# Attention and two dense layers in one program: scores kept negated, fewer small steps, three tiles of each early pair turned by TensorE

## The chip, the cores and the metric

The program runs on one core of a Trainium2 chip. The time is device microseconds for one execution. The core has TensorE (PE; its weight loads are shown apart as PEld), VectorE (DVE), ScalarE (ACT), GpSimd (POOL) and SyncE (SP), which here issues all DMAs. Each engine runs its own instructions in the order in which the program has them; semaphores make one wait for another.

## What is computed

Attention over 4 batches of 8 heads (576 positions, 64 columns a head), in which scores further than `tau` below the row's maximum are dropped, and behind it two dense layers over all 2304 rows (512 to 2048 and back), the first with `s * relu(h)^2 + b`, the second with `h * sigmoid(1.702 h)`:

```python
scores = scale * np.matmul(q, k.transpose(0, 1, 3, 2))
thresh = np.max(scores, axis=-1, keepdims=True) - tau
scores = np.where(scores >= thresh, scores, -1000000000.0)
scores = scores - np.max(scores, axis=-1, keepdims=True)
attn = np.exp(scores)
attn = attn / (np.sum(attn, axis=-1, keepdims=True) + 1e-09)
x = np.matmul(attn, v)                      # then heads side by side
g = s * np.maximum(x @ w_in, 0.0) ** 2 + b  # first layer, x = g @ w_out
h = x @ w_in2; out = (h / (1.0 + np.exp(-1.702 * h))) @ w_out2
```

## The kernel before

*Attention.* Two heads make a pair; 16 pairs, four to a batch, each with nine score tiles of 128 rows (`tile_step`, tile 8 holds the last 64 rows of both heads). TensorE multiplies a tile's scores into a PSUM buffer `S` of 128x576, of which there are three while the first batch runs, two later. VectorE takes the row's negated maximum (`nm`, line 511) and derives from it `tb`, the bound below which a score is dropped (line 516), and `nb`, the bias of the exponential (line 522). ScalarE computes `e = exp(S + nb)` (line 529). VectorE masks it with `S >= tb` and sums the row in the same instruction (line 533), after which `S` is free. ScalarE rounds `e` to 16 bits (`p16`, line 324), GpSimd puts the rest into the second half of `p16` (lines 542 and 543), and SP issues a DMA transpose of `p16` into `PT` (line 545). With all nine tiles of a pair turned, TensorE multiplies them with the values (`finish_main`, line 605, `finish_last`, line 646) into a PSUM buffer `T`, which is also used for smaller transposes; there are two of these in the first batch. Values are scaled by a power of two for each head (`prep_v`, lines 444 to 450: reduction, four small steps on `vm`, two copies into `vcol`, reciprocal).

*Dense layers.* All matmuls of the two layers write `y` (line 788 for the hidden rows, 851 for the projection). The weights arrive as 64-bit numbers and are first converted (`convert`: ScalarE, three instructions on VectorE, one on GpSimd for each block of 128 rows). The first batch's rows of the first layer run with 32-bit matmuls, the others with three products of shorter ones. The layers of a batch start as soon as that batch's attention is done, and run interleaved with the attention of the later batches; from about 710 us on only `y` matmuls are left on TensorE.

*What sets the order.* Every step is put into a `Plan` with its engine, an estimated cost, its buffers and a priority from a table of constants `KN` (times at which parts are due, and leads in us). `Plan.run` goes through the steps in order of time and gives each free engine the ready step of the lowest priority value; the resulting order is written out as it is. What SP, VectorE, ScalarE, GpSimd and TensorE do one after another is thus fixed when the program is built.

Of the kernel before, what the change touches and what calls it, by code (L numbers as in the profile page):

```python
# [9 lines left out]
F32 = mybir.dt.float32  # L10
F32R = mybir.dt.float32r
F16 = mybir.dt.float16
# [14 lines left out]
R = 9  # L27
# [17 lines left out]
    "spread": 8,  # L45
}

# [22 lines left out]
class Plan:  # L70
# [50 lines left out]
    def run(self, engines):  # L121
        steps = self.steps
        for op in steps:
            op["left"] = len(op["after"])
            for a in op["after"]:
                steps[a]["then"].append(op["n"])
        slots = {k: q[0].bufs for k, q in self.turns.items()}
        next_turn = dict.fromkeys(self.turns, 0)
# [3 lines left out]
        clock = Clock()  # L132
        for seg in range(self.segment + 1):
# [7 lines left out]
            while count < len(todo):  # L141
# [4 lines left out]
                while ends and ends[0][0] <= now:  # L146
                    for b in steps[heapq.heappop(ends)[1]]["bufs"]:
                        b.users -= 1
                        if b.users == 0:
                            slots[id(b.pool), b.tag] += 1  # L150
                moved = False
                for e in engines:
# [3 lines left out]
                    while ready[e]:  # L156
# [12 lines left out]
                        need = {}  # L169
                        ok = True  # L170
                        new = sorted((b for b in op["bufs"] if not b.live), key=lambda b: b.turn)
                        for b in new:
                            k = (id(b.pool), b.tag)
                            i = need.get(k, 0)
                            if b.turn != next_turn[k] + i or slots[k] <= i:
                                ok = False
                                break
                            need[k] = i + 1
                        if not ok:
                            put.append((p, n))  # L180
                            continue
                        for b in new:
                            b.live = True
                        for k, i in need.items():
                            next_turn[k] += i
                            slots[k] -= i
                        op["start"], op["on"] = now, e
# [94 lines left out]
class Kernel:  # L282
# [9 lines left out]
    def consts(self, pool):  # L292
        nc = self.nc
        self.ident = pool.tile([P, P], F32, name="ident")
        make_identity(nc, self.ident)
        sc = pool.tile([P, 3], F32, name="scal")
# [12 lines left out]
        self.under = pool.tile([P, 1], F32, name="under")  # L309
        nc.vector.tensor_tensor(self.under, t1, t2, ALU.add)  # L310
# [44 lines left out]
    def ps(self, tag, shape):  # L355
# [5 lines left out]
        return Buf(self.pa if own else self.px, tag, shape, F32, n if own else more)  # L361
# [55 lines left out]
    def prep_v(self, p):  # L417
# [24 lines left out]

        def scales(_):
# [7 lines left out]
        add({"DVE": 1085.0}, scales, [T], [vm, vs, vcol])  # L451
# [11 lines left out]
    def tile_step(self, p, i):  # L463
# [38 lines left out]
        else:  # L502
# [4 lines left out]
        tb = self.at("tb", [P, 1], F32, bufs=4)  # L507
# [3 lines left out]
            {"DVE": 668.0}, lambda _: nc.vector.tensor_reduce(nm.ap, Sv(), AX.XY, ALU.max, negate=True), [Sp], [nm],  # L511
# [3 lines left out]
            {"DVE": 130.0},  # L515
            lambda _: nc.vector.tensor_scalar(tb.ap, nm.ap, -1.0, self.under, ALU.mult, ALU.subtract), [nm], [tb],  # L516
            prio=self.plan.prio - KN["tb"] * pace,
        )
        nb = self.at("nb", [P, 1], F32, bufs=4)
        add(  # L520
            {"DVE": 130.0},
            lambda _: nc.vector.tensor_scalar(nb.ap, nm.ap, LOG_SP, None, ALU.add), [nm], [nb],
            prio=self.plan.prio - KN["tb"] * pace - 1.0,
# [5 lines left out]
            lambda _: nc.scalar.activation(ev(), Sv(), AF.Exp, bias=nb.ap, scale=1.0), [Sp, nb], [e],  # L529
# [4 lines left out]
                ev(), Sv(), tb.ap, ev(), ALU.is_ge, ALU.mult, accum_out=p["acc"][:, i, 0:1]  # L534
            ),
            [Sp, tb, e], [e, (p["acc"], i)], prio=self.plan.prio - KN["sc"] * pace,
# [8 lines left out]
        add({"SP": (1360.0, 1800.0, 1280.0)}, lambda _: nc.sync.dma_start_transpose(pt(), p16.ap), [p16], [(PT, part)], turns=True)  # L545
# [116 lines left out]
    def attention(self, pairs):  # L662
# [3 lines left out]
        for n, p in enumerate(pairs):  # L666
# [3 lines left out]
            def do(step, p, i):  # L670
                at = pairs[n]["start"] + pairs[n]["pace"] * i / R
                plan.prio, self.lending = at, p["lend"]
                step(p)

            if n == 0:
                do(self.prep_qk, p, 0)
            p["PT"] = {}
# [23 lines left out]
    def heads(self, b, start, pace, lend=False):  # L701
        return [
            {
                "b": b, "hp": hp, "start": start + hp * pace, "pace": pace, "lend": lend,
                "parts": b * NP + hp >= KN["parts"], "spread": b * NP + hp >= KN["spread"],
            }
            for hp in range(NP)
        ]
# [383 lines left out]
```

## Time and profile before

| what | us |
|---|---|
| median of 3 runs | 1100.98 (1099.6 to 1103.26) |
| the profiled execution | 1097.05 |
| its span in the trace | 1095.2 |
| TensorE busy in the span | 1034.4 |
| VectorE busy in the span | 810.4 |
| ScalarE busy in the span | 675.6 |

The page's busy time of TensorE counts a matmul from its start to its modelled end, at whatever clock it ran. The table of stretches gives for each engine how long it was busy in a window, the number of instructions in brackets, and the granted clock as a share of the full 2.4 GHz. The list of waits gives an engine and a line, and the engine and line whose end ended the wait. The timeline's first two columns are start and duration in us.

### The profile page before, as it was taken

To read this page: it belongs to the slowest core of one execution; us is meant where nothing else is said; L and a number is where in the kernel's file an instruction comes from. 1 tells how busy PE (TensorE), PEld (TensorE's weight loads), DVE (VectorE), ACT (ScalarE), POOL (GpSimd) and SP (SyncE) were. 2 spreads that over 40 slices of the span, in tenths; PEclk is the share of its full clock that TensorE was granted. 3 is DMA by queue.
4 is the path that set the end of the run, shared out by engine and by line. 5 is a ranking of instruction groups with operands and counts; after the bars stand their busy time and mean duration, and the time that the engine had idled before them with its cause. 6 is when DMAs were issued, how large, how long until landed. Compare 5 with 4: busy or idle time off the path is not lost.

```text
span 1095.2 us, 16161 instructions
## 1 busy us (share of the span) xinstructions
PE 1034.4 (94%) x5264; PEld 754.5 (69%) x5264; DVE 810.4 (74%) x1727; ACT 675.6 (62%) x1216; POOL 430.6 (39%) x477
## 2 busy tenths in 40 slices
PE   3777889999999999999999999999999999999998
PEld 1333334445678777878877787868888888888886
DVE  6999798999898988999998878765444544444443
ACT  5776778778988765776666587655655433223221
POOL 2765565757775577556556343500000000000000
PEclk7777899999999998999999999999999999999999
DMA  7999899898988656768576866542211112020102
GB/s 220 202 188 225 217 244 247 211 255 239 227 197 227 165 136 171 204 170 223 139 187 162 198 171 145 127 139 78 78 60 66 30 49 68 1 68 10 54 34 67
DMA packets 228756, 161.54 MB, mean 147 GB/s; under 512 B 180728, under 2 KB 181312, under 8 KB 228672
## 3 DMA queue, kind: packets, MB, share of 16 engines
q1 hardware_dynamic: 228672, 160.52, 57.3%
q8 instruction: 41, 0.67, 0.3%
q14 instruction: 43, 0.35, 0.1%
HBM read 93.85 MB, written 24.15 MB: 108 GB/s over the span
## 4 chain that ended last, share of the span: by engine, by line
PE 56%; DVE 6%; issue 2%; ACT 1%; DMA 1%; SPq 0%; POOL 0%; DVEq 0%; ACTq 0%; POOLq 0%
PE y L851 27%; PE y L788 26%; PE S L490 2%; PE T L605 1%; DVE e L533 1%; DVE ww L749 1%; DVE nm L511 1%; DVE gl L339 1%; DVE ww L738 0%; DVE wl L339 0%; DMA wst<-in_moe_w_in 0%; DVE accb L864 0%; DVE wa L742 0%; DMA raw<-in_q 0%; DVE gt L816 0%
## 5 line engine op out<-in xcount | busy, mean ns | idle before, releaser
L542 POOL TENSOR_TENSOR p<-e,p 128x512 f16<-128x512 f32 x123 | 151.3, 1230 | 150.7 <-ACT p L324 122.1
L788 PE MATMUL y<-xa,wh 128*128 128x512 f32 x512 | 183.8, 453 | 0.0
L788 PE MATMUL y<-xb,wh 128*128 128x512 f32 x512 | 164.0, 401 | 0.4 <-DVE xb L339 0.4
L851 PE MATMUL y<-gh,wh 128*128 128x512 f32 (+1 forms) x384 | 156.1, 449 | 3.3 <-POOL wh L759 2.0
L529 ACT ACTIVATE e<-S,nb 128x576 f32<-128x576 f32 x144 | 104.3, 733 | 46.0 <-DVE tb L516 19.9
L533 DVE SCALAR_TENSOR_TENSOR e<-S,tb,e 128x576 f32<-128x576 f32 x144 | 115.8, 808 | 15.3 <-ACT e L529 14.3
L788 PEld LDWEIGHTS y<-xa,wh 128*128 128x128 f32 x512 | 94.0, 190 | 43.4 <-issue 26.7
L851 PE MATMUL y<-wh,gh 128*128 128x512 f32 x288 | 115.6, 401 | 3.7 <-DVE gt L816 3.7
L511 DVE TENSOR_REDUCE nm<-S 128x1 f32<-128x576 f32 x144 | 106.4, 745 | 14.5 <-PE S L497 8.0
L851 PE MATMUL y<-wl,gh 128*128 128x512 f32 x288 | 114.4, 397 | 0.0
L851 PE MATMUL y<-wh,gl 128*128 128x512 f32 x288 | 114.3, 397 | 0.0
L813 ACT ACTIVATE gt<-y 128x512 f32<-128x512 f32 (+1 forms) x80 | 44.2, 553 | 111.1 <-PE y L788 111.0
L339 DVE TENSOR_TENSOR gl<-gt,gh 128x512 fp32r<-128x512 f32 (+1 forms) x134 | 99.4, 757 | 17.7 <-ACT gh L324 17.0
L788 PEld LDWEIGHTS y<-xb,wh 128*128 128x128 f32 x512 | 94.9, 189 | 24.5 <-DVE xb L339 1.3
L816 DVE SCALAR_TENSOR_TENSOR gt<-gt,y 128x512 f32<-128x512 f32 (+1 forms) x80 | 50.4, 630 | 75.7 <-ACT gt L813 75.7
L788 PE MATMUL y<-xb,wl 128*128 128x512 f32 x256 | 101.6, 397 | 0.0
L324 ACT ACTIVATE p<-e 128x576 f16<-128x576 f32 x123 | 82.8, 678 | 30.5 <-DVE e L533 20.7
L339 POOL TENSOR_TENSOR gl<-gt,gh 128x512 fp32r<-128x512 f32 (+1 forms) x10 | 11.9, 1190 | 222.0 <-DVE gh L320 220.8
L851 PEld LDWEIGHTS y<-gh,wh 128*128 128x128 f32 x384 | 70.7, 189 | 37.1 <-issue 23.2
L851 PE MATMUL y<-gl,wh 128*128 128x512 f32 (+1 forms) x256 | 93.8, 366 | 0.5 <-POOL gl L339 0.5
L851 PE MATMUL y<-gh,wl 128*128 128x512 f32 (+1 forms) x256 | 93.8, 366 | 0.0
L324 ACT ACTIVATE wh<-wl 128x512 fp32r<-128x512 f32 x104 | 64.1, 626 | 33.6 <-DMA wl<-wd 32.2
(138 smaller groups left out, 2193.1 us busy)
## 6 DMA issues: line engine op xcount, KB each, us to landing
wl<-wd SPq DMA_DIRECT2D x128, 256.0 KB, 2.9
wst<-in_moe_w_in SPq DMA_DIRECT2D x32, 512.0 KB, 4.7
wst<-in_moe_w_out SPq DMA_DIRECT2D x32, 512.0 KB, 5.0
wd<-wh SPq DMA_DIRECT2D x32, 256.0 KB, 4.2
wd<-ww SPq DMA_DIRECT2D x32, 256.0 KB, 2.1
raw<-in_k SPq DMA_DIRECT2D x16, 288.0 KB, 3.1
raw<-in_q SPq DMA_DIRECT2D x16, 288.0 KB, 3.0
rv<-in_v SPq DMA_DIRECT2D x14, 320.0 KB, 5.5
```

Of the source, the lines that this page charges most:

```text
L324: nc.scalar.activation(dst(), src(), AF.Copy)
L339: engines, lambda e: self.eng[e].tensor_tensor(dst(), a(), b(), ALU.subtract), reads, writes, **kw
L490: nc.tensor.matmul(Sp[:, half, :HALF], q[h][j][:, qcols[h]], k[h][:, half * HALF : (half + 1) * HALF], start=(h, j) == (heads[0][0], 0), s ...
L511: {"DVE": 668.0}, lambda _: nc.vector.tensor_reduce(nm.ap, Sv(), AX.XY, ALU.max, negate=True), [Sp], [nm],
L529: lambda _: nc.scalar.activation(ev(), Sv(), AF.Exp, bias=nb.ap, scale=1.0), [Sp, nb], [e],
L533: lambda _: nc.vector.scalar_tensor_tensor(ev(), Sv(), tb.ap, ev(), ALU.is_ge, ALU.mult, accum_out=p["acc"][:, i, 0:1]),
L542: nc.gpsimd.tensor_tensor(p16[:, S + H2 :], e[:, :MAIN], p16[:, :MAIN], ALU.subtract)
L605: nc.tensor.matmul(Up[h * H2 : (h + 1) * H2, :], V[:, h, slot, :], p["PT"][h][:, j, :], start=start, stop=stop)
L788: nc.tensor.matmul(hp(), wt[:, kk * P : (kk + 1) * P], xv(j, kk), start=(i == 0), stop=(i == len(terms) - 1))
L813: add({"ACT": act(n, True)}, lambda _: nc.scalar.activation(t(), hp(), AF.Tanh, scale=0.851), [hps], [gt])
L816: lambda _: nc.vector.scalar_tensor_tensor(t(), t(), 1.0, hp(), ALU.add, ALU.mult), [hps, gt], [gt],
L851: nc.tensor.matmul(yp(), a, b, start=(i == 0), stop=(i == len(terms) - 1))
```

## The change

The scores are kept negated: the scale of `k` has the other sign, so the row's minimum is taken, the exponential gets a scale of -1, and the mask asks `<=`. Bias and bound come from one instruction: a constant tensor `both` of 128x3 (bias, bound, zero) plus the row's minimum gives `nb`, of which column 0 is the bias and column 1 the bound. The scaling of values takes both heads in one instruction, and the copies into `vcol` move to GpSimd. In each pair of the first batch, tiles 1, 8 and 6 (by `TURNS[1]`, twelve tiles in all) are turned by TensorE: nine 128x128 transposes of 16-bit numbers into two `T` buffers, five and four, each copied to `PT` by ScalarE. `s` and `b` are loaded behind the first pair's loads, a `warm` activation is added on ScalarE, and an identity of 16 bits on GpSimd. The table `KN` has other numbers, which move instructions on all engines, and `Plan.run` keeps a step that waits for a buffer aside until one comes free.

```diff
-    "lead": 6, "boost": 30, "mix": 14, "ahead": 10, "t0": 59.94, "t1": 186.71, "t2": 461.81, "t3":
+    "lead": 2, "boost": 45, "mix": 14, "ahead": 4, "t0": 57.56, "t1": 186.71, "t2": 430.13, "t3":
...
+TURNS = ((), (1, 8, 6), (0, 2, 8, 5, 7), (8,), (1, 6))
...
-        for i, src in enumerate((self.tau, self.s, self.b)):
-            nc.sync.dma_start(sc[:, i : i + 1], src.partition_broadcast(P))
-        self.s_ap, self.b_ap = sc[:, 1:2], sc[:, 2:3]
+        nc.sync.dma_start(sc[:, :1], self.tau.partition_broadcast(P))
+        self.warm = pool.tile([P, 1], F32, name="warm")
+        nc.scalar.activation(self.warm, self.ident[:, :1], AF.Exp)
...
-        nc.vector.tensor_scalar(self.qs, z, 1.0 / math.sqrt(D), None, ALU.mult)
+        nc.vector.tensor_scalar(self.qs, z, -1.0 / math.sqrt(D), None, ALU.mult)
...
+        self.both = pool.tile([P, 3], F32, name="both")
+        nc.vector.memset(self.both, 0.0)
+        nc.vector.tensor_scalar(self.both[:, 0:1], t2, 0.0, LOG_SP, ALU.mult, ALU.add)
+        nc.vector.tensor_tensor(self.both[:, 1:2], t1, t2, ALU.add)
+
+    def layer_consts(self):
+        for i, src in enumerate((self.s, self.b)):
+            self.nc.sync.dma_start(self.sc[:, i + 1 : i + 2], src.partition_broadcast(P))
...
         def scales(_):
-            nc.vector.tensor_reduce(vm.ap, T.ap, AX.X, ALU.max)
-            for h in range(2):
-                m, rows = vm[:, h : h + 1], slice(h * H2, (h + 1) * H2)
-                nc.vector.tensor_scalar(m, m, 2.0 ** -113 / unit, unit, ALU.max, ALU.mult)
-                nc.vector.tensor_scalar(m.bitcast(I32), m.bitcast(I32), 0x7F800000, None, ALU.bitwise_and)
-                nc.vector.tensor_copy(vcol[rows], m[rows])
-            nc.vector.reciprocal(vs.ap, vm.ap)
+            m = vm.ap.bitcast(I32)
+            nc.vector.tensor_scalar(vm.ap, vm.ap, 2.0 ** -113 / unit, unit, ALU.max, ALU.mult)
+            nc.vector.tensor_scalar(m, m, 0x7F800000, None, ALU.bitwise_and)
+            nc.vector.reciprocal(vs.ap, vm.ap)
+        add({"DVE": 450.0}, scales, [vm], [vm, vs])
+
+        def col(e):
+            for h in range(2):
+                rows = slice(h * H2, (h + 1) * H2)
+                self.eng[e].tensor_copy(vcol[rows], vm[rows, h : h + 1])
+        add({"POOL": 300.0}, col, [vm], [vcol])
...
-            {"DVE": 668.0}, lambda _: nc.vector.tensor_reduce(nm.ap, Sv(), AX.XY, ALU.max, negate=True), [Sp], [nm],
+            {"DVE": 668.0}, lambda _: nc.vector.tensor_reduce(nm.ap, Sv(), AX.XY, ALU.min), [Sp], [nm],
...
-            lambda _: nc.vector.tensor_scalar(tb.ap, nm.ap, -1.0, self.under, ALU.mult, ALU.subtract), [nm], [tb],
+            lambda _: nc.vector.tensor_scalar(nb.ap, self.both, nm.ap, None, ALU.add), [nm], [nb],
...
-            lambda _: nc.vector.tensor_scalar(nb.ap, nm.ap, LOG_SP, None, ALU.add), [nm], [nb],
...
-            lambda _: nc.scalar.activation(ev(), Sv(), AF.Exp, bias=nb.ap, scale=1.0), [Sp, nb], [e],
+            lambda _: nc.scalar.activation(ev(), Sv(), AF.Exp, bias=nb[:, 0:1], scale=-1.0), [Sp, nb], [e],
...
-                ev(), Sv(), tb.ap, ev(), ALU.is_ge, ALU.mult, accum_out=p["acc"][:, i, 0:1]
+                ev(), Sv(), nb[:, 1:2], ev(), ALU.is_le, ALU.mult, accum_out=p["acc"][:, i, 0:1]
...
+        for some in (range(KS), range(KS, R)):
+            T = self.ps("T", [P, KS, P], F16)
+
+            def turn(_, some=some, T=T):
+                for j in some:
+                    nc.tensor.transpose(T[:, j - some[0], :], p16[:, j * P : (j + 1) * P], self.ident16)
+            add({"PE": (len(some) * 60.0 + 100.0, 60.0)}, turn, [p16], [T])
+            self.copy(
+                lambda some=some: pt()[:, some[0] : some[-1] + 1], lambda some=some, T=T: T[:, : len(some)], [T],
+                [(PT, (part, some[0]))], len(some) * P, psum=True, also=0,
+            )
```

Three places show what moves. SP's queue at the very start, before:

```order
L298 DMA scal<-in_tau 128x1
L298 DMA scal<-in_moe_s 128x1
L298 DMA scal<-in_moe_b 128x1
L343 DMA kk<-in_k 128x576
L343 DMA qa<-in_q 128x576
L343 DMA qb<-in_q 128x576
```

and SP's queue at the same place in the changed program:

```order
L311 DMA scal<-in_tau 128x1
L366 DMA kk<-in_k 128x576
L366 DMA qa<-in_q 128x576
L366 DMA qb<-in_q 128x576
L366 DMA rv<-in_v 128x640
L333 DMA scal<-in_moe_s 128x1
L333 DMA scal<-in_moe_b 128x1
```

The two loads of one number now stand behind the four large ones of the first pair.

VectorE in the first pair, around the masks of its sixth and seventh tile, before (`nm` is the row's maximum, `e` the masked exponential, `ww` and `wa` steps of a weight's conversion):

```order
L511 TENSOR_REDUCE nm_277<-S_255 128x1
L742 TENSOR_SCALAR wa_205<-ww_266 128x65x8
L522 TENSOR_SCALAR nb_285<-nm_277 128x1
L516 TENSOR_SCALAR tb_287<-nm_277,under_87 128x1
L533 SCALAR_TENSOR_TENSOR e_279,acc_110<-S_225,tb_275,e_279 128x576
L511 TENSOR_REDUCE nm_292<-S_270 128x1
L533 SCALAR_TENSOR_TENSOR e_290,acc_110<-S_255,tb_287,e_290 128x576
L522 TENSOR_SCALAR nb_304<-nm_292 128x1
L516 TENSOR_SCALAR tb_306<-nm_292,under_87 128x1
```

and VectorE there in the changed program, from the mask of the seventh tile on:

```order
L557 SCALAR_TENSOR_TENSOR e_281,acc_114<-S_255,nb_277,e_281 128x576
L541 TENSOR_REDUCE nm_298<-S_284 128x1
L541 TENSOR_REDUCE nm_306<-S_291 128x1
L546 TENSOR_SCALAR nb_314<-both_89,nm_298 128x3
L546 TENSOR_SCALAR nb_322<-both_89,nm_306 128x3
L541 TENSOR_REDUCE nm_324<-S_301 128x1
L784 TENSOR_SCALAR wa_203<-ww_273 128x65x8
L546 TENSOR_SCALAR nb_341<-both_89,nm_324 128x3
L557 SCALAR_TENSOR_TENSOR e_326,acc_114<-S_284,nb_314,e_326 128x576
```

Each tile has one small instruction where there were two, and reductions stand further ahead of the masks.

ScalarE at the end of the first pair, before (`e` the exponential of a tile's scores, `gt` and `p16` its 16-bit copy, `wa` a weight's conversion):

```order
L529 ACTIVATE e_315<-S_270,nb_304 128x576
L732 ACTIVATE wa_329<-wst_138 128x64x8
L733 ACTIVATE wa_329<-ident_70 128x8
L529 ACTIVATE e_333<-S_296,nb_325 128x576
L324 ACTIVATE gt_340<-e_315 128x576
L324 ACTIVATE gt_349<-e_333 128x576
```

and ScalarE there in the changed program (`T` is what TensorE has turned of the fifth tile):

```order
L347 ACTIVATE p16_304<-e_281 128x576
L553 ACTIVATE e_326<-S_284,nb_314 128x576
L347 ACTIVATE PTm_333<-T_316 128x640
L347 ACTIVATE PTm_333<-T_328 128x512
L553 ACTIVATE e_344<-S_291,nb_322 128x576
L347 ACTIVATE gt_348<-e_326 128x576
```

The two copies of turned numbers stand between the exponentials of the eighth and the ninth tile.

## Rows read from the trace of the kernel before

**Rows 1.** The page: span, and busy time (share of span) of each engine.

```profile
span 1095.2 us, 16161 instructions
PE 1034.4 (94%) x5264; PEld 754.5 (69%) x5264; DVE 810.4 (74%) x1727; ACT 675.6 (62%) x1216; POOL 430.6 (39%) x477
```

**Rows 2.** Table of stretches: window, length, engines' busy time, TensorE's clock, DMA share, GB/s.

```profile
0.00:20.00 20.00, 6.80 (x30) 3.35 (x30) 10.35 (x33) 10.10 (x18) 3.87 (x12) 0.89 0.69 235
20.00:113.00 93.00, 69.15 (x443) 32.84 (x442) 89.51 (x269) 68.74 (x118) 60.30 (x82) 0.73 0.93 203
113.00:160.00 47.00, 41.07 (x165) 17.00 (x164) 39.32 (x96) 36.25 (x69) 26.46 (x32) 0.89 0.90 234
160.00:345.00 185.00, 181.82 (x831) 101.74 (x830) 168.12 (x362) 154.63 (x287) 122.19 (x130) 1.00 0.90 230
345.00:720.00 375.00, 365.45 (x1906) 289.40 (x1905) 330.87 (x668) 253.44 (x450) 210.71 (x217) 0.99 0.69 172
720.00:1095.00 375.00, 370.16 (x1896) 310.19 (x1894) 172.24 (x304) 152.47 (x279) 7.03 (x7) 1.00 0.17 53
```

**Rows 3.** Timeline, the last matmul.

```profile
1090.13 0.40 PE L851 MATMUL y<-wl,gh 128*128 128x512 f32 x1
```

**Rows 4.** Waits from 20 to 113 us: total us, times, longest.

```profile
PE S L497 <- DVE e L533: 13.8, 13, 2.1
ACT e L529 <- DVE tb L516: 12.0, 11, 3.4
```

**Rows 5.** Stretches again, VectorE's instructions that write or read `nm`.

```profile
0.00:20.00 20.00, 4.24 (x11) 0.89 0.69 235
20.00:113.00 93.00, 34.92 (x117) 0.73 0.93 203
```

**Rows 6.** Timeline of the start: `s` and first `k`, table load, first scores.

```profile
1.18 0.42 SPq L298 DMA_DIRECT2D scal<-in_moe_s  x1
...
2.12 0.43 SPq L343 DMA_DIRECT2D kk<-in_k  x1
...
6.49 1.28 ACT L379 ACT_TABLE_LOAD   x1 [6.49 <-DMA kk<-in_k]
...
8.61 3.25 PE L497 MATMUL S<-kk,qa 64*128 64x288 f32 x12 [8.61 <-ACT kk L379]
```

**Rows 7.** Timeline, VectorE, the two small steps of a tile and their successor.

```profile
31.60 0.15 DVE L522 TENSOR_SCALAR nb<-nm 128x1 f32<-128x1 f32 x1
31.67 0.21 DVE L516 TENSOR_SCALAR tb<-nm,under 128x1 f32<-128x1 f32 x1
31.79 0.17 DVE L552 TENSOR_REDUCE ri<-acc 128x9 f32<-128x18 f32 x1
```

**Rows 8.** Timeline, VectorE, the first step on `vm` and the successor of the last.

```profile
37.24 0.15 DVE L447 TENSOR_SCALAR vm<-vm 128x1 f32<-128x1 f32 x1
...
38.29 0.80 DVE L533 SCALAR_TENSOR_TENSOR e<-S,tb,e 128x576 f32<-128x576 f32 x1
```

**Rows 9.** Who waited for the DMA transposes of line 545 (us, times), whole run.

```profile
  PE T L605: 1.6, 2
...
  ACT p L324: 0.5, 1
```

**Rows 10.** A copy out of PSUM (grouped, 20 to 113 us); two groups of matmuls (timeline).

```profile
L324 ACT ACTIVATE rs<-T 64x512 f32<-64x512 f32 x8 | 4.7, 588 | 1.1 <-PE T L580 0.9
...
720.36 0.63 PE L646 MATMUL T<-PTm,V 128*64 128x64 f16 x28
...
132.96 0.60 PE L580 MATMUL T<-ident,ri 128*64 128x128 f32 x4
```

**Rows 11.** Timeline, GpSimd, the larger step of a tile's low part.

```profile
139.21 1.16 POOL L542 TENSOR_TENSOR p<-e,p 128x512 f16<-128x512 f32 x1 [1.36 <-issue]
```

**Rows 12.** Timeline, scores of one tile at the upper and the lower clock.

```profile
118.70 0.76 PE L497 MATMUL S<-kk,qb 64*128 64x288 f32 x4
...
125.18 1.33 PE L497 MATMUL S<-kk,qa 64*128 64x288 f32 x4 [1.73 <-DVE e L533]
```

More of the change, by code (lines that the diff above doesn't have):

```diff
@@ L40 @@
 KN = {
[4 rows of a table removed]
-    "spread": 8,
[4 rows of a table added]
+    "turns": 1, "tn": 4, "spread": 8,
 }
+TURNS = ((), (1, 8, 6), (0, 2, 8, 5, 7), (8,), (1, 6))
 class Buf:
@@ L126, in run @@
                 steps[a]["then"].append(op["n"])
+            op["keys"] = [((id(b.pool), b.tag), b) for b in sorted(op["bufs"], key=lambda b: b.turn)]
         slots = {k: q[0].bufs for k, q in self.turns.items()}
+        blocked = {k: [] for k in slots}
         next_turn = dict.fromkeys(self.turns, 0)
@@ L132, in run, with again @@
         clock = Clock()
+        def again(k):
+            for e, p, n in blocked[k]:
+                heapq.heappush(ready[e], (p, n))
+            blocked[k].clear()
         for seg in range(self.segment + 1):
@@ L146, in run @@
                 while ends and ends[0][0] <= now:
-                    for b in steps[heapq.heappop(ends)[1]]["bufs"]:
+                    for k, b in steps[heapq.heappop(ends)[1]]["keys"]:
                         b.users -= 1
                         if b.users == 0:
-                            slots[id(b.pool), b.tag] += 1
+                            slots[k] += 1
+                            again(k)
                 moved = False
@@ L168, in run @@
                                 continue
[L169 to L173, printed above, removed]
+                        need, stuck = {}, None
+                        for k, b in op["keys"]:
+                            if b.live:
+                                continue
                             i = need.get(k, 0)
                             if b.turn != next_turn[k] + i or slots[k] <= i:
-                                ok = False
+                                stuck = k
                                 break
                             need[k] = i + 1
-                        if not ok:
-                            put.append((p, n))
+                        if stuck:
+                            blocked[stuck].append((e, p, n))
                             continue
-                        for b in new:
+                        for k, b in op["keys"]:
                             b.live = True
@@ L186, in run @@
                             slots[k] -= i
+                            again(k)
                         op["start"], op["on"] = now, e
@@ L295, in consts @@
         make_identity(nc, self.ident)
+        self.ident16 = pool.tile([P, P], F16, name="ident16")
+        nc.gpsimd.tensor_copy(self.ident16, self.ident)
         sc = pool.tile([P, 3], F32, name="scal")
-        for i, src in enumerate((self.tau, self.s, self.b)):
-            nc.sync.dma_start(sc[:, i : i + 1], src.partition_broadcast(P))
-        self.s_ap, self.b_ap = sc[:, 1:2], sc[:, 2:3]
+        nc.sync.dma_start(sc[:, :1], self.tau.partition_broadcast(P))
+        self.warm = pool.tile([P, 1], F32, name="warm")
+        nc.scalar.activation(self.warm, self.ident[:, :1], AF.Exp)
+        self.s_ap, self.b_ap, self.sc = sc[:, 1:2], sc[:, 2:3], sc
         z = pool.tile([P, 1], F32, name="z")
@@ L308, in consts @@
         nc.vector.tensor_scalar(t2, sc[:, 0:1], 0.0, None, ALU.max)
-        self.under = pool.tile([P, 1], F32, name="under")
-        nc.vector.tensor_tensor(self.under, t1, t2, ALU.add)
+        self.both = pool.tile([P, 3], F32, name="both")
[5 more added lines that the diff above has]
+            self.nc.sync.dma_start(self.sc[:, i + 1 : i + 2], src.partition_broadcast(P))
     def copy(self, dst, src, reads, writes, cols, scale=None, psum=False, also=0, **kw):
@@ L353, in at, with ps @@
         return Buf(self.ap, tag, shape, dt, bufs)
-    def ps(self, tag, shape):
+    def ps(self, tag, shape, dt=F32):
         n, more = {"S": (2, 1), "T": (1, 1)}[tag]
@@ L360, in ps @@
         own = i % (n + more) < n
-        return Buf(self.pa if own else self.px, tag, shape, F32, n if own else more)
+        return Buf(self.pa if own else self.px, tag, shape, dt, n if own else more)
     def prep_qk(self, p):
@@ L441, in prep_v @@
         vs = self.at("vs", [P, 2], F32)
+        add(
+            {"DVE": dve(256, psum=True) + 60}, lambda _: nc.vector.tensor_reduce(vm.ap, T.ap, AX.X, ALU.max), [T], [vm]
+        )
         def scales(_):
-            nc.vector.tensor_reduce(vm.ap, T.ap, AX.X, ALU.max)
-            for h in range(2):
-                m, rows = vm[:, h : h + 1], slice(h * H2, (h + 1) * H2)
-                nc.vector.tensor_scalar(m, m, 2.0 ** -113 / unit, unit, ALU.max, ALU.mult)
-                nc.vector.tensor_scalar(m.bitcast(I32), m.bitcast(I32), 0x7F800000, None, ALU.bitwise_and)
-                nc.vector.tensor_copy(vcol[rows], m[rows])
-            nc.vector.reciprocal(vs.ap, vm.ap)
-        add({"DVE": 1085.0}, scales, [T], [vm, vs, vcol])
+            m = vm.ap.bitcast(I32)
[4 more added lines that the diff above has]
+        def col(e):
+            for h in range(2):
+                rows = slice(h * H2, (h + 1) * H2)
+                self.eng[e].tensor_copy(vcol[rows], vm[rows, h : h + 1])
+        add({"POOL": 300.0}, col, [vm], [vcol])
         for h in range(2):
@@ L514, in tile_step @@
         add(
-            {"DVE": 130.0},
-            lambda _: nc.vector.tensor_scalar(tb.ap, nm.ap, -1.0, self.under, ALU.mult, ALU.subtract), [nm], [tb],
+            {"DVE": 150.0},
+            lambda _: nc.vector.tensor_scalar(nb.ap, self.both, nm.ap, None, ALU.add), [nm], [nb],
             prio=self.plan.prio - KN["tb"] * pace,
[L518 to L521, printed above, removed]
-            lambda _: nc.vector.tensor_scalar(nb.ap, nm.ap, LOG_SP, None, ALU.add), [nm], [nb],
-            prio=self.plan.prio - KN["tb"] * pace - 1.0,
         )
@@ L544, in tile_step @@
         add({"POOL": Shared(pool(MAIN) + pool(H2))}, low, [e, (p16, 0)], [(p16, 1)])
-        add({"SP": (1360.0, 1800.0, 1280.0)}, lambda _: nc.sync.dma_start_transpose(pt(), p16.ap), [p16], [(PT, part)], turns=True)
+        if i not in p["turns"]:
+            add(
+                {"SP": (1360.0, 1800.0, 1280.0)}, lambda _: nc.sync.dma_start_transpose(pt(), p16.ap), [p16], [(PT, part)],
+                turns=True,
+            )
+            return
+        for some in (range(KS), range(KS, R)):
[7 more added lines that the diff above has]
+                [(PT, (part, some[0]))], len(some) * P, psum=True, also=0,
+            )
     def finish_sums(self, p):
@@ L676, in attention @@
                 do(self.prep_qk, p, 0)
+                plan.add({"SP": 1040.0}, lambda _: self.layer_consts(), prio=1.0)
             p["PT"] = {}
@@ L703, in heads @@
             {
+                "turns": TURNS[KN["turns"]] if b * NP + hp < KN["tn"] else (),
                 "b": b, "hp": hp, "start": start + hp * pace, "pace": pace, "lend": lend,
```

4 lines of the change are left out of this document (2 added, 2 removed), and 6 rows, old and new, of the table KN.

## The prediction

> **What bounds the kernel now.** I read the page's first line, then the table of stretches, then who waits for whom inside the stretch that looked worst, and last the timeline at the places that the change touches. TensorE is busy for 1034.4 of 1095.2 us [rows 1], so the span is TensorE's work plus its idle time plus what it loses to the lower clock. The stretches say where that is [rows 2]. After 160 us TensorE idles 3.2 us up to 345, 9.6 us up to 720 and 4.8 us to the end, of which the last sum and the stores after the last matmul take 4.7 (the last matmul ends at 1090.53) [rows 3]. Before 160 us it idles 13.2 us (0 to 20), 23.9 us (20 to 113) and 5.9 us (113 to 160), at a granted clock of 0.89, 0.73 and 0.89 against 1.00 later. Whatever this change gives must come from there, about 43 us of idle time and some slow matmuls.
>
> In 20 to 113 us VectorE is busy for 89.5 of 93 us, and what TensorE waits for there is the score buffer that VectorE's masking step frees (13.8 us in 13 waits) [rows 4]. ScalarE's exponentials wait for VectorE's small step `tb` (12.0 us) [rows 4]. So the first stretch is VectorE's. By 113 us some 42 of the 144 score tiles have been reduced (11 + 117 instructions on `nm`, three for each tile) [rows 5]. From 113 to 345 us it is mixed: TensorE is nearly full (222.9 of 232 us), VectorE at 207.4 of 232 [rows 2].
>
> **The change, part by part.** The profiled execution took 1097.05 us and its span is 1095.2; the median of the runs shown is 1100.98, 3.9 us more. I sum against 1097.05 and add the 3.9 at the end.
>
> *Head.* The loads of `s` and `b` leave the front of SP's queue. They were issued at 1.18 and 1.64, and `kk` behind them at 2.12 [rows 6]; `kk` can now go at about 1.18, 0.94 us earlier. The chain from it is single: landing, table load, scaling, first scores at 8.61 [rows 6]. The new `warm` activation, which would take the 1.28 us table load out of that chain, stands in ScalarE's program behind the table load and the first `kk` scaling, and the table load still waits for the same DMA, so I give it nothing. Head: -0.9 us.
>
> *Small steps.* `nb` starts at 31.60, `tb` at 31.67, the next instruction at 31.79: the pair holds VectorE for 0.19 us [rows 7]. One step with a tensor operand remains; no row shows it. Its ends are 0.07 us (like `nb`) and 0.19 us (nothing saved). I take 0.12, the time from `tb` to its successor, because `tb` too reads an operand from memory: 0.07 us saved for each tile. Keeping the scores negated is free: the reduction and the mask keep shape and source.
>
> *Scales.* Behind the reduction of `vm` come seven small instructions from 37.24 until the next one starts at 38.29: 1.05 us [rows 8]. Three remain, each on the result of the one before: 3 of 7 by count, 0.45 us. Saved 0.6 us for each pair of heads. The two copies to `vcol` go to GpSimd, which has 32.7 us idle in 20 to 113 [rows 2], and are read a pair later.
>
> To tile 42 this is 42 x 0.07 + 5 x 0.6 = 5.9 us of VectorE. The order of the program moves conversions of weights around that: ahead of tile 37 it now has eight more of them (about 0.7 to 0.8 us each), ahead of tile 43 the same number as before. So tile 37 is not earlier, and tile 43 can be, by 5.9 us.
>
> *Turns.* Twelve of the first 36 transposes go from SP's DMA to TensorE. What that removes costs nothing in this trace: all that waited for a DMA transpose in the whole run is 1.6 us on TensorE and 0.5 us on ScalarE [rows 9], although the DMA engines are 93% busy there. What it adds: 108 transposes on TensorE, and 24 copies out of PSUM on ScalarE, 640 and 512 columns. For the copies the nearest row is `rs<-T`, 588 ns for 512 columns out of PSUM [rows 10]; 640 columns by proportion 735 ns. Together 12 x 1.32 = 15.9 us on a ScalarE that is busy for 68.7 of 93 us: 84.6 of then 87. That is as full as VectorE (89.5 - 5.9 = 83.6 of 87). For the transposes the bounds are 0.02 us each (28 small 16-bit matmuls in 0.63 us) and 0.15 us (four 32-bit ones in 0.60) [rows 10], so 2 to 16 us. TensorE idles 23.9 us there, which covers either, but a turn stands ahead of a later tile's scores in TensorE's queue, and its copy stands ahead of a later tile's exponential in ScalarE's. Without cover each turned tile would cost up to 1.32 us of ScalarE plus 0.2 to 1.35 us of TensorE.
>
> With two engines at 96 and 97% in one chain I don't believe in the whole 5.9 us. Bounds for 20 to 113 are -5.9 and, if every turn holds the chain for 1 us, +6; I take -3, the middle of no loss and all lost, because ScalarE's idle time (24.3 us) is still more than the copies.
>
> *113 to 345 us.* Program orders agree in TensorE's work up to the 88th tile (308 and 302 projection matmuls ahead of it). VectorE has 46 x 0.07 + 5 x 0.6 = 6.2 us less. TensorE can use at most its idle time there, 9.1 us. Bounds 0 and -9; since VectorE has 24.6 us idle of its own there [rows 2] and is not the only limit, I take -3.
>
> *Behind 345 us.* The retuned table moves later tiles: by the 118th tile TensorE has 180 more projection matmuls behind it (1184 against 1004) and at the last both meet at the same point, 1616, with the same four groups of 12 between the last scores and the last pair's mixing. TensorE's 9.6 + 4.8 us of idle time could shrink or grow by some 4; I take 0.
>
> Sum: -0.9 - 3 - 3 + 0 = -6.9, so **1090 us** for a profiled execution and **1094 us** for the median.
>
> **The rivals.** *A, VectorE alone counts.* If ScalarE's copies fit into its waits for `tb`, the head gives 0.9, tile 42 the full 5.9 and the next stretch 8 of its 9.1 us: -14.8, 1086 us. For it: VectorE is the only engine at 96% now. Against: ScalarE near 97% afterwards.
>
> *B, ScalarE takes VectorE's place.* The 15.9 us of copies eat what VectorE saved until tile 42, and the middle stretch is TensorE's anyway: -0.9 and a loss of the same size, 1101 us. For it: ScalarE's sum above. It decides when the stretch from 20 to the 42nd tile stays at 93 us.
>
> *C, slower: turns block TensorE's queue.* In order, a turn waits for GpSimd's low part of its tile and for a free T buffer, of which there are two, each held until ScalarE has copied it; behind the turn stand the next tile's scores, behind these VectorE's reduction. At 1.4 us for each of 12 turned tiles this costs 16.8 us and the gain of 6.9 becomes +10: 1111 us. It decides from 0.6 us a turned tile. Against it: the order puts each turn three to five tiles behind its own tile. At three, with three score buffers, the tile's mask may only just be done when the turn comes up, and a copy and the low part, whose larger step alone takes 1.16 us on GpSimd [rows 11], are still to come; but the next scores must wait for the next mask in any case, and a tile takes 93 / 39 = 2.4 us.
>
> *D, the clock.* One tile's scores take 0.76 us in a stretch at 2.4 GHz and 1.33 us at 1.2 GHz [rows 12]; the granted clock of 20 to 113 us is 0.73, so about half of that stretch ran at either level. If turns brought the upper level to none of the first 36 tiles, 36 x 0.5 x 0.57 = 10 us more would stand on TensorE, of which its idle time covers about half: +5 on -6.9, 1099 us. The Trainium skill, page "TensorE: Matmul & The Clock Gate", Part 4 (PE-mode transpose), says that transposes do not count as busy work for the clock, which is the mechanism of D; by it the time would be 1099 and by the row alone, where more matmuls stand in the same time, 1094. No row here shows a 16-bit transpose.
>
> **How the numbers follow.** A measurement of this kernel can tell about 0.3%, 3.3 us, from no change: faster means below 1097.7, slower above 1104.3. My forecast has a chance of 0.50 and a range of its own of 1089 to 1099; about a tenth of it lies in no change. A 0.15, B 0.18, C 0.12, D 0.05. Faster: 0.45 of the forecast, 0.15 of A, 0.03 of B and D, together 0.63. Same: 0.05 + 0.13 of B + 0.04 of D = 0.22. Slower: 0.12 of C and 0.03 of B = 0.15. The range of 8 in 10 runs from somewhat under A, where all bounds on the good side meet (-0.9 - 5.9 - 9.1 - 3, 1082), to the near side of C: 1082 to 1106.
>
> **What the profile afterwards would show.** Head right: first scores near 7.7 instead of 8.61. Steps right: one `nb` of 128x3 that holds VectorE for about 0.12 us; three small steps on `vm`. First stretch right: the 43rd reduction at about 109 instead of 113, with ScalarE over 90% busy until the last turn. B shows as VectorE waiting for `e` by ScalarE, C as waits of TensorE on line 580 for GpSimd or ScalarE, D as a lower granted clock than 0.73. The middle is right if TensorE's idle time before 345 us falls by about 6 us, and the rest if its idle time from there on stays at about 14 us. The forecast fails if the last does not hold: an order that leaves TensorE short of work between 345 and 720 us undoes everything ahead of it.

## The result, and the profile after

The changed kernel takes 1117.17 us in the median of four runs (1113.48 to 1119.84), the kernel before 1101.36 beside it: a ratio of 1.0141, interval 1.0101 to 1.0181. It is slower, and the predicted 1094, with a range up to 1106, was wrong. The profiled execution took 1113.48 us, its span is 16.5 us longer than that of before.

The page's first lines (span; busy time of each engine), to be held against [rows 1]:

```profile
span 1111.7 us, 16133 instructions
...
PE 1041.4 (94%) x5372; PEld 769.8 (69%) x5372; DVE 828.1 (74%) x1516; ACT 686.9 (62%) x1238; POOL 452.0 (41%) x518
```

VectorE has 211 instructions fewer and is busy 17.7 us longer. TensorE is busy 7.0 us longer and idle for 1111.7 - 1041.4 = 70.3 us where it was 60.8: 9.5 us more. The two make up the 16.5.

The table of stretches, with the columns of [rows 2]:

```profile
0.00:20.00 20.00, 8.88 (x41) 4.53 (x41) 12.10 (x33) 11.18 (x20) 5.71 (x18) 1.00 0.76 259
20.00:113.00 93.00, 68.16 (x515) 40.52 (x517) 86.18 (x200) 77.55 (x137) 57.52 (x85) 0.82 0.70 158
113.00:160.00 47.00, 45.00 (x200) 19.12 (x195) 42.42 (x86) 37.55 (x70) 27.52 (x36) 1.00 0.90 216
160.00:345.00 185.00, 174.03 (x797) 96.70 (x798) 167.48 (x301) 150.88 (x281) 128.37 (x140) 1.00 0.90 229
345.00:720.00 375.00, 361.11 (x1867) 288.34 (x1866) 339.27 (x579) 248.31 (x443) 224.80 (x234) 0.99 0.65 168
```

TensorE loses from 160 to 345 us (174.0 busy, 181.8 before) and from 345 to 720 (361.1, 365.5); from 113 to 160 us it is busier than before (45.0, 41.1). VectorE has fewer instructions and is hardly less busy from 160 to 345 us, and busier behind it: 339.3 us for 579 instructions from 345 to 720 us, 330.9 for 668 before. So single instructions have become longer.

Which ones, the grouped instructions show (x count, then busy us and mean ns of one). After:

```profile
L546 DVE TENSOR_SCALAR nb<-both,nm 128x3 f32<-128x3 f32 x144 | 63.9, 449 | 0.7
L472 DVE TENSOR_SCALAR vm<-vm 128x2 f32<-128x2 f32 x16 | 7.2, 449 | 0.0
L473 DVE TENSOR_SCALAR vm<-vm 128x2 int32<-128x2 int32 x16 | 5.7, 354 | 0.6
```

and before:

```profile
L516 DVE TENSOR_SCALAR tb<-nm,under 128x1 f32<-128x1 f32 x144 | 28.7, 201 | 0.0
L522 DVE TENSOR_SCALAR nb<-nm 128x1 f32<-128x1 f32 x144 | 20.5, 142 | 0.6
L448 DVE TENSOR_SCALAR vm<-vm 128x1 int32<-128x1 int32 x32 | 4.9, 154 | 1.1
```

One step of three columns takes 449 ns, two of one column took 142 and 201 (part of each overlaps its neighbour). The step itself is not long. The instructions of line 546 alone (shortest, median, longest ns), and ScalarE's exponential behind them:

```profile
L546 DVE TENSOR_SCALAR nb<-both,nm x144: 168/228/1379, 9.9 to 719.0; 128x3 f32<-128x3 f32 x144
...
  ACT e L553: 37.7, 41
```

ScalarE's waits for the step, 37.7 us, are hardly above those of before (19.9 us for `tb` and 16.7 for `nb`, 36.6 together), so what the step costs is VectorE's own time.

What the long ones have in common is seen in the timeline (start, duration, idle before), VectorE and GpSimd at 31 us:

```profile
31.45 1.28 POOL L801 TENSOR_TENSOR wh<-wh,wst 128x512 int32<-128x512 int32 x1
31.61 0.22 DVE L593 RECIPROCAL ri<-ri 128x9 f32<-128x9 f32 x1
31.75 1.02 DVE L546 TENSOR_SCALAR nb<-both,nm 128x3 f32<-128x3 f32 x1
32.68 0.80 DVE L557 SCALAR_TENSOR_TENSOR e<-S,nb,e 128x576 f32<-128x576 f32 x1
```

GpSimd's instruction ends at 32.73, the small step at 32.77. In the whole trace 86 of the 144 steps started while a GpSimd instruction ran or within 0.01 us ahead of one, with a mean of 602 ns; 82 of these ended within 0.13 us behind the end of a GpSimd instruction, nearly always the one they had met. The longest, 1.38 us, did not: it began 0.1 us ahead of the end of one and lasted until the next had ended. The 58 others took 222 ns. The one-column steps of before take 142 and 201 ns whatever GpSimd does.

How it reaches TensorE is seen from 361 us on, where `y` waits 4.74 us, the longest of its waits:

```profile
361.11 1.76 DVE L362 TENSOR_TENSOR gl<-gt,gh 128x512 fp32r<-128x512 f32 x1
...
362.89 1.71 DVE L421 SCALAR_TENSOR_TENSOR kk<-raw,qs,kk 64x576 fp32r<-64x576 f32 x1
...
363.95 1.77 POOL L362 TENSOR_TENSOR wl<-ww,wh 128x512 fp32r<-128x512 f32 x1
...
364.63 1.11 DVE L546 TENSOR_SCALAR nb<-both,nm 128x3 f32<-128x3 f32 x1
365.66 0.68 DVE L906 TENSOR_TENSOR accb<-y,accb 128x512 f32<-128x512 f32 x1
...
366.40 1.22 PE L830 MATMUL y<-xb,wh 128*128 128x512 f32 x2 [4.74 <-DVE accb L906]
```

The small step holds VectorE until GpSimd is done, and the sum that frees TensorE's buffer stands behind it. Of the 4.74 us the small step answers for some 0.9 (1.11 against 0.22 where GpSimd is idle); the two larger steps ahead of it, which the kernel before has too, took 1.76 and 1.71 us where such steps take 0.86 and 1.06 in the mean of this trace.

### The profile page after: what moved, and what is told of

Same layout as the page of the kernel before. It is cut to its first block, busy times and chain, and to the rows that moved or that the text cites. A ratio compares the mean times of both kernels' runs of the same rounds, so it can differ in the third digit from the quotient of the medians.

```text
span 1111.7 us, 16133 instructions
## 1 busy us (share of the span) xinstructions
PE 1041.4 (94%) x5372; PEld 769.8 (69%) x5372; DVE 828.1 (74%) x1516; ACT 686.9 (62%) x1238; POOL 452.0 (41%) x518
## 5 line engine op out<-in xcount | busy, mean ns | idle before, releaser
L362 POOL TENSOR_TENSOR gl<-gt,gh 128x512 fp32r<-128x512 f32 (+1 forms) x15 | 18.1, 1206 | 363.0 <-DVE gh L343 352.9
L553 ACT ACTIVATE e<-S,nb 128x576 f32<-128x576 f32 x144 | 105.8, 736 | 56.5 <-DVE nb L546 37.7
L557 DVE SCALAR_TENSOR_TENSOR e<-S,nb,e 128x576 f32<-128x576 f32 x144 | 115.8, 808 | 12.1 <-ACT e L553 11.9
L362 DVE TENSOR_TENSOR gl<-gt,gh 128x512 fp32r<-128x512 f32 (+1 forms) x129 | 96.3, 762 | 15.9 <-ACT gh L347 15.2
L347 ACT ACTIVATE wh<-wl 128x512 fp32r<-128x512 f32 x109 | 67.3, 625 | 39.1 <-DMA wl<-wd 38.3
```

Source lines behind the costliest of these rows:

```text
L347: nc.scalar.activation(dst(), src(), AF.Copy)
L362: engines, lambda e: self.eng[e].tensor_tensor(dst(), a(), b(), ALU.subtract), reads, writes, **kw
L553: lambda _: nc.scalar.activation(ev(), Sv(), AF.Exp, bias=nb[:, 0:1], scale=-1.0), [Sp, nb], [e],
L557: lambda _: nc.vector.scalar_tensor_tensor(ev(), Sv(), nb[:, 1:2], ev(), ALU.is_le, ALU.mult, accum_out=p["acc"][:, i, 0:1]),
```

## The experiments

Theory W: the wide small steps wait for GpSimd. Theory O: the order from the new table loses. The first four runs tell them apart; before took 1099.86 us beside them.

**Two one-column steps in the place of the wide one**, order unchanged:

```diff
-            lambda _: nc.vector.tensor_scalar(nb.ap, self.both, nm.ap, None, ALU.add), [nm], [nb],
+            nc.vector.tensor_scalar(nb[:, 0:1], nm.ap, LOG_SP, None, ALU.add)
+            nc.vector.tensor_scalar(nb[:, 1:2], nm.ap, self.both[:, 1:2], None, ALU.add)
```

> The changed kernel, with one thing undone: the step that makes bias and bound issues two instructions of one column each, in place of one of three columns. The order of all other instructions stays. In the changed kernel's trace the three-column step takes 0.45 us in the mean and up to 1.38, and is long where GpSimd is in the middle of an instruction; the one-column steps of the kernel before took 0.14 and 0.20 whatever GpSimd did. Theory W (the wide step waits for GpSimd, and that is most of the loss): the step's total falls from 64 us to some 40 in overlapped durations with none over 0.25 us, and the time falls by 7 to 13 us, to a ratio of 1.002 to 1.008 against the kernel before. Theory O (the twelve turned tiles and the new order make the loss, the wait only fills idle time): the steps get short, and the ratio stays at 1.011 to 1.016.

1099.44 us, ratio 1.0001 (0.9987 to 1.0015). The whole loss is gone, more than the 7 to 13 us expected, with the table, the turns and all else in place. Its two steps:

```profile
L542 DVE TENSOR_SCALAR nb<-nm,both 128x1 f32<-128x1 f32 x144 | 28.8, 201 | 0.0
L541 DVE TENSOR_SCALAR nb<-nm 128x1 f32<-128x1 f32 x144 | 20.5, 142 | 0.7
```

**The scales' steps one column wide as well:**

```diff
-            nc.vector.tensor_scalar(vm.ap, vm.ap, 2.0 ** -113 / unit, unit, ALU.max, ALU.mult)
+            for h in range(2):
+                m = vm[:, h : h + 1]
+                nc.vector.tensor_scalar(m, m, 2.0 ** -113 / unit, unit, ALU.max, ALU.mult)
```

(and the masking of exponents likewise.)

> As e1, and the two steps on the scales of values are one column each again too (four instructions for two, the copies stay on GpSimd). In the changed kernel these two-column steps took 0.45 and 0.35 us against 0.15. W: 3 us less on VectorE than e1, 1 to 2 us less in time. O: as e1.

1098.28 us, 0.9978 (0.9954 to 1.0001): 1.2 us less than with the wide scales, too little to be told apart.

**One step still, but of nine columns**, read from rows of four and written without gaps:

```diff
-        nb = self.at("nb", [P, 3], F32, bufs=4)
+        nb = self.at("nb", [P, 9], F32, bufs=4)
-            lambda _: nc.vector.tensor_scalar(nb.ap, self.both, nm.ap, None, ALU.add), [nm], [nb],
+            lambda _: nc.vector.tensor_scalar(nb.ap, self.both[:, :, :3], nm.ap, None, ALU.add), [nm], [nb],
```

(`both` is now 128x3x4.)

> The changed kernel with one wide step for bias and bound as before, but of nine columns that are read as three rows of three out of four, and written in one piece, so that the outermost lengths of source and destination differ (3 and 9). W, in the form that the wait comes from VectorE using its second port, shared with GpSimd, whenever the shapes let it: no wait, each step 0.17 to 0.25 us although it has three times the columns, and a time like e1 or up to 3 us under it. If the wait came from the number of columns or from the operand in memory, it is as long as in the changed kernel, with the ratio at 1.011 to 1.016.

1098.48 us, 0.9977 (0.9955 to 0.9999). Three times the columns, and it never waits (shortest, median, longest):

```profile
L546 DVE TENSOR_SCALAR nb<-both,nm x144: 161/215/226, 9.8 to 706.5; 128x9 f32<-128x9 f32 x144
```

So it isn't the merging that is dear but the form. The Trainium skill, page "VectorE: DVE Perf Modes", section "Mode 2×_2P", says that a one-source step in SBUF goes through both read ports if the outermost length is even, or odd and equal on both sides: 3 and 3 in the change, 3 and 9 in this run. By the Trainium skill, page "SBUF — State Buffer", section "Who interferes with whom", the second pair of ports is shared with GpSimd under a lock that one holds for its whole instruction. The traces fit both: 82 of 86 steps end with a GpSimd instruction, and the one of nine columns does not wait. That the ports are the reason is not shown beyond that: this run changes the lengths, the gaps in what is read and the number of columns together.

**The kernel before, with only its bias step three columns wide:**

```diff
-            lambda _: nc.vector.tensor_scalar(nb.ap, nm.ap, LOG_SP, None, ALU.add), [nm], [nb],
+            lambda _: nc.vector.tensor_scalar(nb.ap, self.both, nm.ap, None, ALU.add), [nm], [nb],
```

> The kernel before, in its own order, with one thing added: the bias step writes three columns from a constant of three columns, as in the change; the bound keeps its own one-column step. W: the bias step gets 0.3 us longer in the mean, 45 us more on VectorE, of which some 17 in the first 113 us; the time grows by 10 to 25 us (ratio 1.010 to 1.022). O: VectorE's idle time takes it, ratio under 1.005.

1125.24 us, 1.0235 (1.0204 to 1.0265): one wider step makes the old kernel slower than the change did, a little more than the 1.010 to 1.022 expected.

```profile
L524 DVE TENSOR_SCALAR nb<-both,nm 128x3 f32<-128x3 f32 x144 | 68.6, 476 | 0.6
...
L518 DVE TENSOR_SCALAR tb<-nm,under 128x1 f32<-128x1 f32 x144 | 28.9, 201 | 0.0
```

W stands, and O is no cause of the loss.

**Table and turns, without the waits.** The next four have the nine-column step and one-column scales, and cross the table (new or before's) with the turns (on, or off by `"tn": 0`). Before took 1099.84 us.

> The changed kernel without any step that waits for GpSimd: bias and bound in nine columns of unequal shapes (as e3) and the scales of values in one-column steps. New table of constants, twelve tiles turned by TensorE. With e5, e6 and e8 it makes a square: new or old table, tiles turned or not. Without the waits VectorE has about 10 us less work to the 42nd tile than the kernel before in its sum; e3 came to a ratio of 0.998. Expected here: 0.994 to 0.999, 1 to 3 us under e3.

> As e7, but no tile is turned by TensorE: all 144 go by DMA again. The order is made anew from the same table. Theory P (the turned tiles cost: 16 us of copies on ScalarE, nothing gained, since in the kernel before 2 us of waits in all were for DMA transposes): 2 to 6 us faster than e7. Theory Q (the turned tiles pay, since the DMA engines were 93% busy there and the copies lie in ScalarE's waits): 2 to 6 us slower than e7.

> As e5, but with the table of constants of the kernel before. What is left of the change is the code: negated scores, one step for bias and bound, fewer steps for scales, the head. P and the sum of the prediction for these parts (0.9 at the head, 5.9 to the 42nd tile, 3 behind it): ratio 0.990 to 0.995. If the new table is what pays: the ratio is 0.997 to 1.003 and e5 is lower.

> As e6 with the twelve tiles turned by TensorE. P: 2 to 6 us slower than e6. Q: 2 to 6 us faster than e6.

| table | turns | us | ratio |
|---|---|---|---|
| new | on | 1094.91 | 0.9957 (0.9938 to 0.9976) |
| new | off | 1104.43 | 1.0047 (1.0028 to 1.0066) |
| before's | off | 1108.90 | 1.0079 (1.0061 to 1.0096) |
| before's | on | 1105.81 | 1.0059 (1.0038 to 1.0079) |

The first has the changed kernel's order on every engine, so the way from 1.4% slower to 0.4% faster is the waits alone; it beats both kernels. The turns were expected to move the time by 2 to 6 us one way or the other: it is 9.5 us with the new table and 3.1 with the old one, both in their favour. The third row misses both its ranges (0.990 to 0.995, 0.997 to 1.003): it has less work than the kernel before and is 0.8% slower. Its stretch behind 345 us, against 365.45 of TensorE in [rows 2]:

```profile
345.00:720.00 375.00, 355.88 (x1838) 280.50 (x1837) 322.56 (x588) 245.48 (x438) 224.41 (x233) 0.99 0.63 170
```

VectorE has 8.3 us less to do there and TensorE is idle 19.1 us instead of 9.6. The last three have orders that the planner made anew, from other steps and costs, so neither the edit in the old order nor the turns had been measured alone. Two more runs keep an order instruction by instruction; before took 1099.77 us.

**Before's order, with the merged step put in its place:**

```diff
-            lambda _: nc.vector.tensor_scalar(tb.ap, nm.ap, -1.0, self.under, ALU.mult, ALU.subtract), [nm], [tb],
+            lambda _: None, [nm], [tb],
-            lambda _: nc.vector.tensor_scalar(nb.ap, nm.ap, LOG_SP, None, ALU.add), [nm], [nb],
+            lambda _: nc.vector.tensor_scalar(nb.ap, self.both[:, :, :3], nm.ap, None, ALU.add), [nm], [nb],
```

(The scores are negated too, and `nb` has eight buffers instead of four.)

> The kernel before with its order kept instruction by instruction, and only this edit: scores negated, bias and bound from one step of nine columns (the shape that does not wait for GpSimd) at the place of the old bias step, nothing at the place of the old bound step. In the run with the new table and the turns this step held VectorE for 0.150 us (21.6 us for 144) where the two of before held it for 0.201 (28.9 us), so 0.05 us are saved for each tile. Theory S (the step saves what it saves, and the +0.8% of the run with before's table and no turns comes from the order that the planner made anew from other costs): 42 tiles x 0.05 = 2.1 us where VectorE is the bound, and up to as much again until 345 us: 1096 to 1099 where before takes 1100, ratio 0.996 to 0.999. Theory N (an earlier exponential moves other waits, the edit itself loses): ratio above 1.003.

1097.93 us, 0.9986 (0.9972 to 1.0000): 1.8 us. The edit without the wait gains about what 42 tiles of 0.05 us give, and does not lose. So the 0.8% lay in the new order or in what this run leaves out (scales, copies to `vcol` on GpSimd, the head). These parts are in the first row of the table too, where nothing is lost, which speaks for the order; they were not tried in the old order.

**The best one's order, its twelve turned tiles through the DMA again:**

```diff
-                for j in some:
-                    nc.tensor.transpose(T[:, j - some[0], :], p16[:, j * P : (j + 1) * P], self.ident16)
+                if some[0] == 0:
+                    nc.sync.dma_start_transpose(pt(), p16.ap)
```

(and no copies.)

> The kernel with the new table and the turns (1094.91, ratio 0.9957), with its order kept on every engine, but its twelve turned tiles go through the DMA transpose again: 108 transposes on TensorE and 24 copies on ScalarE are gone, and 12 DMA transposes are issued by SP, each at the place of the first turn of its tile. Theory Q (what the turns remove is worth the gain: 12 x 1.31 us of SP's queue, in which all loads of weights stand, and DMA time): 5 to 9 us slower than with the turns, 1100 to 1104, ratio 1.000 to 1.004, with waits for late loads. Theory R (the turns cost something and the gain lay in the order that the planner made around them): as fast or faster, 1088 to 1095, ratio 0.989 to 0.996, since 15.9 us of ScalarE and some 12 us of TensorE are saved.

1096.95 us, 0.9975 (0.9960 to 0.9989), between the two theories: with the turns it was 0.9957, and the intervals overlap. In place the turns are worth some 2 us, by the two intervals from -1 to 5, so not clear of nothing. Most of the 9.5 us between the first two rows of the table is in the order around them: this run and the second row do the same work in two orders, and are 0.7% apart. Which piece of the order it is was not isolated.

**GpSimd's instructions in quarters.** Each of 512 columns becomes four of 128 in the same step, in the changed kernel and in the one before.

```diff
-            nc.gpsimd.tensor_tensor(p16[:, S + H2 :], e[:, :MAIN], p16[:, :MAIN], ALU.subtract)
+            self.quarters("POOL", p16[:, S + H2 :], e[:, :MAIN], p16[:, :MAIN], ALU.subtract)
```

> The changed kernel with the same order on every engine; only each GpSimd instruction on 512 columns is cut into four on 128 columns, in the same step. A GpSimd instruction of 1.16 to 1.5 us becomes four of some 0.4 to 0.5 us. Theory W (the 128x3 step waits until the GpSimd instruction that runs then ends): the wait can be no longer than one quarter, so the longest of the 144 steps falls from 1.38 us to under 0.7, the mean from 449 ns to about 330 (236 where GpSimd is idle, and a quarter to a half of the 374 more where it runs), and 10 to 17 us of the loss on VectorE come back, less what GpSimd's longer work costs: 1102 to 1112 instead of 1117. Rival V (the step is slower as long as GpSimd runs at all, or two ports cost it time by themselves): mean and longest stay, and the time is 1117 or more.

> The control: the kernel before with the same cut of GpSimd's instructions and its order kept. Its small steps are one column wide and took 142 and 201 ns whatever GpSimd did. Theory W: these two stay as they are, and the time moves only by GpSimd's added fixed cost and by the large steps of VectorE that wait for GpSimd too: within 1% of 1100, and less gain than the changed kernel has from the cut. Rival V: the cut moves both kernels by the same amount.

1139.49 us (1.0353, 1.0325 to 1.0381) and 1133.49 (1.0300, 1.0277 to 1.0322) beside 1100.24: both times missed. The cut costs the kernel before 33 us, since a quarter of `p` took GpSimd 489 ns where the whole took some 1.2 us, and GpSimd is busy 570.9 us instead of 430.6. But the changed kernel is only 0.5% behind its control, where it had been 1.4% behind. The mean of its step fell from 449 to 358 ns (some 330 forecast); the control's are as they were:

```profile
L552 DVE TENSOR_SCALAR nb<-both,nm 128x3 f32<-128x3 f32 x144 | 50.8, 358 | 0.7
```

```profile
L522 DVE TENSOR_SCALAR tb<-nm,under 128x1 f32<-128x1 f32 x144 | 28.8, 202 | 0.0
...
L528 DVE TENSOR_SCALAR nb<-nm 128x1 f32<-128x1 f32 x144 | 20.6, 143 | 0.6
```

The longest did not fall below 0.7 us as forecast: it rose to 3.06. VectorE and GpSimd there:

```profile
35.51 3.06 DVE L552 TENSOR_SCALAR nb<-both,nm 128x3 f32<-128x3 f32 x1
```

```profile
34.91 1.58 POOL L369 TENSOR_TENSOR gt<-e,gt 128x128 f16<-128x128 f32 x4
36.45 0.30 POOL L573 TENSOR_TENSOR gt<-e,gt 128x64 f16<-128x64 f32 x1
36.71 1.57 POOL L369 TENSOR_TENSOR p<-e,p 128x128 f16<-128x128 f32 x4
38.25 0.30 POOL L573 TENSOR_TENSOR p<-e,p 128x64 f16<-128x64 f32 x1
```

Of 112 steps that started while GpSimd ran, 85 ended within 0.13 us behind the end of that instruction and 21 behind that of a later one; this one was passed over until nine of GpSimd's had ended. So W holds as a wait for GpSimd, not as a wait for one instruction only.

## Why the prediction was wrong

**The step that failed is "Small steps"**, its price for the 128x3 instruction. It was bounded by 0.07 and 0.19 us and taken at 0.12; it measured 0.45, with 1.38 at the longest. I made the bounds from [rows 7], which are steps of one column, and those don't wait for GpSimd. The nearest row for what I did not know was another one: before's trace holds a copying step of one shape at two prices (both of VectorE, 128x512 from SBUF to SBUF; the three dear ones began while GpSimd ran, the cheap one did not):

```profile
L320 DVE CAST wh<-ww 128x512 fp32r<-128x512 f32 x3 | 3.5, 1183 | 0.5 <-POOL ww L759 0.5
...
L320 DVE CAST xb<-accb 128x512 fp32r<-128x512 f32 x1 | 0.4, 428 | 0.0
```

An upper end of one GpSimd instruction, 1.16 us [rows 11], would have put the slow side into the range: 144 steps, over half of them begun beside GpSimd. All rivals took VectorE's saving for certain, so none had this cause; C came nearest to the time, by another mechanism.

**Scales.** The same error, with less weight: 16 pairs. Where GpSimd is idle the forecast 0.45 us is right (0.47 from the first small step to the next instruction):

```profile
39.11 0.15 DVE L472 TENSOR_SCALAR vm<-vm 128x2 f32<-128x2 f32 x1
39.30 0.17 DVE L473 TENSOR_SCALAR vm<-vm 128x2 int32<-128x2 int32 x1
39.50 0.17 DVE L474 RECIPROCAL vs<-vm 128x2 f32<-128x2 f32 x1
39.58 0.80 DVE L557 SCALAR_TENSOR_TENSOR e<-S,nb,e 128x576 f32<-128x576 f32 x1
```

On the mean the first two take 449 and 354 ns. In all I had VectorE 19.7 us lighter (144 x 0.07 + 16 x 0.6); it became 17.7 us heavier.

**Head.** Right in kind: the first scores start at 7.08 us, 1.5 earlier where I had 0.9 (the load is issued 0.9 earlier and lands 0.6 sooner after its issue), and the table load still waits for `kk` and stands ahead of `warm`, as the order had shown.

**Turns.** Right in size. The 24 copies take 15.5 us of ScalarE (15.9 forecast), the 108 transposes 12.2 us of TensorE (2 to 16). TensorE waits 2.9 us ahead of turns in the whole run, so rival C did not happen, and in place they are worth some 2 us, near the nothing that I gave them. The line has 63 of the 108; the other 45 take 4.8 us and have no wait ahead of them.

```profile
L580 PE MATMUL T<-ident,gt 128*128 128x128 f16 x63 | 7.4, 271 | 2.9 <-POOL gt L567 1.8 <-DVE xm L694 0.6 <-DVE xa L663 0.3
```

**20 to 113 us.** The 43rd reduction comes at 117.3 us, 4.4 later than before; I had it at about 109. Without the waits, new table, turns on, it comes at 111.8: a gain of 1.1 instead of 3.9. Rival D is out, since the granted clock there is 0.82, not below the 0.73 of before; other runs in the order of before have 0.72 to 0.81 there, so 0.82 is no gain of the change either.

**The middle and the end.** From 113 to 345 us the same order without waits has TensorE busy for 222.7 us, before 222.9; its 88th reduction starts at 335.2 us, 2.9 earlier than before, of which 1.8 were won behind the 43rd. So of the forecast 3 us at most some 2 came. Behind 345 us the prediction wanted TensorE's idle time to stay at about 14 us. It is 21.4 us (before 14.6), and 16.3 in the same order without the waits, so most of that rise is the waits as well. For what a new order does I had put 4 us there; the third row of the table is idle for 26.1 us behind 345 us. That term was too narrow too, though it is not what decided here.

**What was left of the forecast.** With the waits away the change takes 1094.9 us, 0.4% less than before, next to the 1094 that I had, but not by the same terms, so the nearness is luck: the merged step gives 1.8 us (in the old order), the turns some 2, and the new order is not told apart from the rest.

## What to carry to other kernels

Before small steps are merged, look whether the wider form waits for another engine where the narrow ones didn't: find a step of the same kind in the trace that has two prices, and see what ran on GpSimd beside the dear one. A step that saves 0.05 us can cost 1 us, and it is paid on the engine that sets the pace. Where a planner makes the order, try an edit inside the old order first; the order by itself moved this kernel by 0.7%.

## What the hardware showed that was not expected

A VectorE step of 128x3 or 128x2, 0.15 to 0.23 us of work, waits for a running GpSimd instruction; of 128x1, and of 128x9 read as 3 rows of 3 and written flat, it doesn't. Large conversion steps of the same kind (`wa<-ww`, 128x520, read flat and written as 65 rows of 8) took 675 to 697 ns in all 64 cases, 38 of them begun while GpSimd ran, so they don't wait either. Nor does every operation wait: a reciprocal of 128x2 took 165 to 167 ns in all 16 cases of the kernel before, 13 of them begun while GpSimd ran. A waiting step can be passed over by GpSimd instructions that follow each other closely, once for 3.06 us.
